# Block 0's first product in halves of 256 tokens, begun between the first chunks, with the weight pieces pinned behind the chunks' own steps

## The chip, the cores and the metric

The kernel runs on one core of one Trainium2 chip. The time is device microseconds (us) of that core. The four executions in the first measurement lie within 0.2% (733.64 to 735.28 us, the kernel before), so differences of 1 us out of 730 need several rounds on one chip; where an interval is given, it is a 95% interval of a ratio. The profile is one execution; its span is about 1.7 us shorter than the time of the same execution (733.6 against 735.37 us for the kernel before).

The engines have short names in the profile: PE is TensorE (matmuls), PEld its weight loads, DVE is VectorE, ACT is ScalarE, POOL is GpSimd, SP issues transfers.

## The reference

```python
# batch 4, 8 heads, 768 tokens, 64 per head; float32
for t in range(S):                                  # retention, chunked by 128 tokens in the kernel
    state = gamma * state + outer(k[t], v[t])
    y[t] = scale * (q[t] @ state)
x = y.transpose(0, 2, 1, 3).reshape(3072, 512)      # 3072 tokens
h = x @ w_in                                        # 512 -> 2048
out = (h * sigmoid(1.702 * h)) @ w_out              # 2048 -> 512
```

The weights come to the kernel as 64-bit words and are made float32 on the chip, in 32 pieces: 16 of w_in and 16 of w_out. This takes one ACT step and six DVE steps for each piece.

## The kernel before

The 3072 tokens go in six blocks of 512, each fed by four chunks of the retention. Blocks 2 to 5 use a product scheme with fewer multiplications, whose operands are first summed from the weights; blocks 0 and 1 run plainly while the weights are still coming in. TensorE's order is that of the program; the other engines' queues are ordered by a scheduler when the kernel is built.

```python
def narrow(n=1):                     # one piece of weights: 1 step of ACT, 6 of DVE
    for _ in range(n):
        ...
        act.activation(m, hi.bitcast(F32), AF.Abs, scale=2.0 ** 16)
        dve.tensor_scalar(m, m, F64_MOST * 2.0 ** 16, F64_LEAST * 2.0 ** 16, op0=ALU.min, op1=ALU.max)
        dve.tensor_scalar(mu, mu, 3, None, op0=ALU.logical_shift_left)
        dve.scalar_tensor_tensor(hi, hi, 0x80000000, mu, op0=ALU.bitwise_and, op1=ALU.bitwise_or)
        dve.tensor_scalar(mu, hi, 0xFF800000, None, op0=ALU.bitwise_and)
        dve.scalar_tensor_tensor(r, lo, 2.0 ** -52, m, op0=ALU.mult, op1=ALU.mult)
        dve.tensor_add(w, ..., ...)
        fetch()                      # the transfer of a later piece into the freed buffer (4 of them)

# a chunk: turn (transposes q and k, ACT copies them), attend (scores; DVE multiplies by the mask),
# finish (products with state and v; DVE writes x and adds to the state)

def up0(m, f):                       # unit f of 16: 128 of the 2048 features, 512 tokens
    p, ab = divmod(f, 2)
    x = X1 if m else X
    h = ps.tile([P, 2, TH], F32, name="ph", tag="xy"[f % 2])     # two tags, two buffers each
    for c in range(4):
        pe.matmul(h, w, x[:, c // 2:4:2, c % 2, :], start=(c == 0), stop=(c == 3))
    hidden(...)                      # ACT: sigmoid; DVE: product

turn(0)
for j in range(CB):                  # the opening: chunks 0 to 3
    attend(j)
    narrow(1)
    turn(j + 1)
    finish(j)
    narrow(1)
between = chunks(1)[1:]
for f in range(NFF):                 # block 0, with the steps of chunks 4 to 7 in between
    up0(0, f)
    if f < NP or f % 4 == 3:
        narrow(1)
    if between and f >= 2:
        between.pop(0)()
for f in range(NFF):                 # block 1
    up0(1, f)
    narrow(1)
    ...
for f in range(NFF):                 # block 0's second product; its four sums take the same PSUM tags
    down0(f)
    ...
```

## Time and profile before

| | before |
|---|---|
| time, median of 3 | 733.7 us |
| span of the profile (of another execution, which took 735.37 us) | 733.6 us |
| PE busy | 712.6 us (97%) |
| first unit of block 0 on PE | 45.04 us |
| first unit of block 1 | 119.07 us |
| block 0's second product | 174.00 us |

These three starts are the marks by which kernels are compared. From 45 us to the end PE has hardly a hole (busy 184.00 of 184.00 us up to 229 us, then 500.01 of 504.60), so a mark that comes earlier should bring the end earlier by as much. The lines of the page are in the prediction.

### The profile page before, as it was taken

The numbers are of one execution on the slowest core, as the hardware profiler recorded it, in microseconds if no ns is written. First come the engines' busy times: TensorE is split into PE (matmuls) and PEld (weight loads), VectorE is DVE, ScalarE is ACT, GpSimd is POOL, SyncE is SP. The second block draws the span as 40 slices with busy tenths as digits, with TensorE's granted clock in tenths as the row PEclk, the third lists the DMA queues.
The fourth block names the chain that finished last, engine by engine and source line by source line (L and its number), as shares of the span: only waits on it lengthen the run. The fifth ranks groups of instructions, "written<-read, shape, count | busy, mean of one in ns | idle before, by whom it ended". The sixth has DMA issues, their size and how long they took to land.

```text
span 733.6 us, 9285 instructions
## 1 busy us (share of the span) xinstructions
PE 712.6 (97%) x3552; PEld 547.0 (75%) x3552; DVE 359.8 (49%) x611; ACT 127.7 (17%) x209; POOL 136.0 (19%) x127
## 2 busy tenths in 40 slices
PE   4789999999999999999999999999999999999997
PEld 3645554444446888888888888888888888888886
DVE  4999999941002652443553344364345273244251
ACT  3233332210000000332000233000233000133100
POOL 2311000323543223000233100032200140200030
PEclk9989999999999999999999999999999999999999
DMA  9877555310001324300334310234300220100001
GB/s 241 202 177 206 157 153 168 89 30 1 0 0 58 68 47 87 74 1 1 65 54 87 61 23 0 48 57 88 74 11 0 42 46 1 44 1 0 15 1 43
DMA packets 142252, 46.24 MB, mean 63 GB/s; under 512 B 129921, under 2 KB 135553, under 8 KB 142209
## 3 DMA queue, kind: packets, MB, share of 16 engines
q1 hardware_dynamic: 135504, 39.10, 23.9%
q10 hardware_dynamic: 6704, 6.57, 2.7%
q8 instruction: 28, 0.46, 0.3%
q14 instruction: 16, 0.12, 0.1%
HBM read 39.33 MB, written 6.29 MB: 62 GB/s over the span
## 4 chain that ended last, share of the span: by engine, by line
PE 93%; DVE 4%; DMA 1%; issue 0%; ACT 0%; SPq 0%; DVEq 0%
PE pd L394 32%; PE ph L291 15%; PE px L343 15%; PE py L343 11%; PE po L303 7%; PE pa L231 3%; PE py L248 3%; PE pu L261 3%; PE py L244 2%; DMA W<-in_moe_w_in_dram 1%; DVE G L333 1%; PE pt L215 1%; DVE W L187 1%; DVE G L334 0%; DVE W L183 0%
## 5 line engine op out<-in xcount | busy, mean ns | idle before, releaser
L394 PE MATMUL pd<-W,G 128*128 128x256 f32 x1120 | 250.3, 381 | 0.4 <-DVE G L334 0.3
L394 PEld LDWEIGHTS pd<-W,G 128*128 128x128 f32 x1120 | 210.1, 190 | 31.2 <-DVE G L334 1.2
L343 PE MATMUL px<-X,W 128*128 128x256 f32 x512 | 119.0, 379 | 0.0
L343 PEld LDWEIGHTS px<-X,W 128*128 128x128 f32 x512 | 97.3, 190 | 13.2
L343 PE MATMUL py<-X,W 128*128 128x256 f32 x384 | 90.7, 379 | 0.0
L343 PEld LDWEIGHTS py<-X,W 128*128 128x128 f32 x384 | 73.0, 190 | 9.9
L222 POOL TENSOR_TENSOR kd<-kn_in,cold 128x512 f32<-128x512 f32 x13 | 15.0, 1151 | 248.8 <-DMA q_sq<-in_q_dram 126.5
L291 PE MATMUL ph<-X,W 128*128 128x512 f32 x128 | 58.5, 605 | 0.0
L291 PE MATMUL ph<-W,W 128*128 128x512 f32 x128 | 55.1, 592 | 0.0
L335 POOL TENSOR_TENSOR G<-G 128x512 f32<-128x512 f32 x20 | 28.9, 1443 | 111.6 <-DVE G L334 111.6
L234 DVE TENSOR_TENSOR at<-pa,mask 128x512 f32<-128x512 f32 x32 | 20.6, 686 | 58.7 <-PE pa L231 58.7
L291 PEld LDWEIGHTS ph<-W,W 128*128 128x128 f32 x128 | 24.3, 190 | 30.6 <-issue 30.4
L291 PEld LDWEIGHTS ph<-X,W 128*128 128x128 f32 x128 | 23.9, 194 | 26.1 <-issue 25.6
L303 PE MATMUL po<-W,W 128*128 128x512 f32 x96 | 42.5, 592 | 0.0
L278 DVE TENSOR_TENSOR G<-G,sg 128x512 f32<-128x512 f32 x48 | 33.1, 689 | 14.1 <-ACT sg L276 14.1
L276 ACT ACTIVATE sg<-G 128x512 f32<-128x512 f32 x48 | 30.3, 631 | 51.3 <-DVE G L353 30.7
L303 PEld LDWEIGHTS po<-W,W 128*128 128x128 f32 x96 | 18.2, 190 | 23.0 <-issue 23.0
L177 ACT ACTIVATE W<-W 128x512 f32<-128x512 f32 x32 | 21.8, 685 | 54.4 <-DMA W<-in_moe_w_out_dram 30.6
L268 POOL TENSOR_TENSOR state<-state,cold 64x256 f32<-64x256 f32 x32 | 21.2, 663 | 53.1 <-DVE state L270 27.6
L353 DVE TENSOR_TENSOR G<-py,p 128x512 f32<-128x512 f32 x16 | 11.1, 692 | 37.8 <-PE py L343 37.8
L306 DVE COPY o<-po 128x512 f32<-128x512 f32 x4 | 2.8, 692 | 52.7 <-PE po L303 51.2
L276 ACT ACTIVATE sg<-ph 128x512 f32<-128x512 f32 x32 | 19.0, 595 | 51.3 <-PE ph L291 43.3
(87 smaller groups left out, 682.2 us busy)
## 6 DMA issues: line engine op xcount, KB each, us to landing
W<-in_moe_w_in_dram SPq DMA_DIRECT2D x16, 512.0 KB, 4.6
W<-in_moe_w_out_dram SPq DMA_DIRECT2D x16, 512.0 KB, 3.4
v_in<-in_v_dram SPq DMA_DIRECT2D x24, 256.0 KB, 4.0
out_dram<-o ACTq DMA_DIRECT2D x24, 256.0 KB, 2.4
kn_in<-in_k_dram SPq DMA_DIRECT2D x21, 256.0 KB, 3.6
q_sq<-in_q_dram SPq DMA_DIRECT2D x256, 16.0 KB, 1.9
k_sq<-in_k_dram SPq DMA_DIRECT2D x256, 16.0 KB, 1.8
q_in<-in_q_dram SPq DMA_DIRECT2D x8, 256.0 KB, 4.6
```

The costliest lines, as they stand in the source:

```text
L177: act.activation(m, hi.bitcast(F32), AF.Abs, scale=2.0 ** 16)
L231: pe.matmul(p[:, i, hp, :], KT[j][r, hp, :], QT[j][r, hp, :], start=True, stop=True)
L248: pe.matmul(y[i * D:(i + 1) * D, hp, :], vn[:, 2 * hp + i, :], a[:, i, hp, :], start=(not c and hp == 0), stop=(hp == HP - 1), skip_group_ ...
L261: pe.matmul(u[:, hp, :], kd[:, h, :].rearrange("p i d -> p (i d)"), vn[:, h, :].rearrange("p i d -> p (i d)"), start=True, stop=True)
L268: pool.tensor_mul(new[r, :, r], old[r, :, r], cold[r, 2 * H:, None].to_broadcast([D, HP, D]))
L276: act.activation(s, h, AF.Sigmoid, scale=1.702)
L278: dve.tensor_mul(g, h, s)
L291: pe.matmul(h, w, x[:, c // 2:4:2, c % 2, :], start=(c == 0), stop=(c == 3))
L303: pe.matmul(PO[n], g0(p, 2 * half + ab)[:, t0:t0 + P], w, start=(f == 0), stop=(f == NFF - 1))
L335: pool.tensor_sub(g[1], g[1], g[0])
L343: pe.matmul(acc[:, u, :], W1[:, 2 * d + u, sa, c, :], X[:, sb, c, :], start=(start and u == 0 and c == 0), stop=(stop and c == 1), skip_gr ...
L394: pe.matmul(p0[:, n, :], G[:, p, sa, n * P:(n + 1) * P], W2[:, sb, p, :], start=(new and p == 0 and n == 0), stop=(last and p == NP - 1), ...
```

## The change

The intent is to put matmuls of block 0 into PE's holes in the opening. A unit on 512 tokens needs all four chunks; on 256 it needs chunks 0 and 1 only, so half units for three pairs of features can run between the chunks. The pins keep the scheduler from queueing pieces of weights ahead of a chunk's own steps: a pinned instruction may not be queued ahead of what was traced before it on its engine.

```diff
-            act.activation(m, hi.bitcast(F32), AF.Abs, scale=2.0 ** 16)
-            dve.tensor_scalar(m, m, F64_MOST * 2.0 ** 16, F64_LEAST * 2.0 ** 16, op0=ALU.min, op1=ALU.max)
+            tc.keep_in_program_order(act.activation(m, hi.bitcast(F32), AF.Abs, scale=2.0 ** 16))
+            tc.keep_in_program_order(dve.tensor_scalar(m, m, F64_MOST * 2.0 ** 16, F64_LEAST * 2.0 ** 16,
+                                                       op0=ALU.min, op1=ALU.max))
...
-    def up0(m, f):
+    def up0(half, p):
+        h = ps.tile([P, 2, TH], F32, name="ph", tag="xy"[p % 2])
+        for ab in range(2):
+            for c in range(4):
+                w = W1[:, p, (c // 2 if ab == 0 else (3, 2)[c // 2]), c % 2, :]
+                pe.matmul(h[:, ab], w, X[:, 2 * half + c // 2, c % 2, :], start=(ab == 0 and c == 0), stop=(c == 3),
+                          skip_group_check=True)
...
+    units = [(half, p) for p in range(3, NP) for half in range(2)]
     for j in range(CB):
         attend(j)
         narrow(1)
         turn(j + 1)
         finish(j)
         narrow(1)
+        if j:
+            up0(0, j - 1)
     between = chunks(1)[1:]
-    for f in range(NFF):
-        up0(0, f)
-        if f < NP or f % 4 == 3:
+    for n, unit in enumerate([(1, p) for p in range(3)] + units):
+        up0(*unit)
+        if n < NP or n % 2:
             narrow(1)
-        if between and f >= 2:
+        if between:
             between.pop(0)()
```

(Block 1's units are the old ones under the name up1.)

More of the change, by code (lines that the diff above doesn't have):

```diff
@@ L276, in hidden @@
         act.activation(s, h, AF.Sigmoid, scale=1.702)
-        for g, h, s in [(g, h, s)] if not isinstance(g, list) else [(g[i], h[:, i], s[:, i]) for i in range(2)]:
-            dve.tensor_mul(g, h, s)
+        for g, i in g if isinstance(g, list) else [(g, slice(0, 2))]:
+            dve.tensor_mul(g, h[:, i], s[:, i])
     def g0(p, s):
@@ L283, in g0, with up1 @@
         return X[:, 4 + p // 2, p % 2] if p < 6 else G0[:, p % 2]
-    def up0(m, f):
+    def up0(half, p):
[5 more added lines that the diff above has]
+                          skip_group_check=True)
+        if half == 0:
+            hidden(W1[:, p, 4:6].rearrange("p s c f -> p s (c f)"), h)
+        else:
+            hidden([(g0(p, 2 + i), i) for i in range(2)], h)
+    def up1(f):
         p, ab = divmod(f, 2)
-        x = X1 if m else X
         h = ps.tile([P, 2, TH], F32, name="ph", tag="xy"[f % 2])
@@ L290, in up0 @@
             w = W1[:, p, (c // 2 if ab == 0 else (3, 2)[c // 2]), c % 2, :]
-            pe.matmul(h, w, x[:, c // 2:4:2, c % 2, :], start=(c == 0), stop=(c == 3))
-        hidden(G[:, p, ab:4:2, :] if m else [g0(p, ab), g0(p, ab + 2)], h)
+            pe.matmul(h, w, X1[:, c // 2:4:2, c % 2, :], start=(c == 0), stop=(c == 3))
+        hidden(G[:, p, ab:4:2, :], h)
     PO = {}
@@ L462 @@
         narrow(1)
+        if j:
+            up0(0, j - 1)
     between = chunks(1)[1:]
-    for f in range(NFF):
-        up0(0, f)
-        if f < NP or f % 4 == 3:
+    for n, unit in enumerate([(1, p) for p in range(3)] + units):
+        up0(*unit)
+        if n < NP or n % 2:
             narrow(1)
-        if between and f >= 2:
+        if between:
             between.pop(0)()
     for f in range(NFF):
-        up0(1, f)
+        up1(f)
         narrow(1)
```

## The prediction

> **What bounds the kernel now.** I read the page first (busy shares, the 40 slices, the chain that ended last), then the stretches table of the first 229 us, then the start in order of time for each engine. First the page:
>
> ```profile
> PE 712.6 (97%) x3552; PEld 547.0 (75%) x3552; DVE 359.8 (49%) x611; ACT 127.7 (17%) x209; POOL 136.0 (19%) x127
> ...
> PE   4789999999999999999999999999999999999997
> ...
> DVE  4999999941002652443553344364345273244251
> ```
>
> TensorE (PE) is the bound: only 733.6 - 712.6 = 21.0 us of the span are without it, and the slices put nearly all of that into the first three slices (18.3 us each). There the VectorE (DVE) row reads 9. So only the opening can be won, and 21 us (2.9%) is the ceiling of any change to it. The stretches table (bounds, length, then busy us and count for PE, PEld, DVE, ACT, POOL, then the granted clock, DMA share and GB/s) says which engine fills which stretch:
>
> ```profile
> 18.20:27.40 9.20, 6.96 (x74) 5.75 (x73) 9.11 (x18) 1.77 (x3) 3.18 (x4) 1.00 0.92 210
> 27.40:33.60 6.20, 4.19 (x39) 3.26 (x38) 6.11 (x13) 2.47 (x4) 2.23 (x3) 1.00 0.65 159
> 33.60:43.30 9.70, 6.92 (x56) 5.32 (x54) 9.42 (x18) 2.25 (x4) 2.94 (x3) 0.85 0.74 180
> ...
> 45.00:119.00 74.00, 74.00 (x330) 39.77 (x329) 72.86 (x156) 23.00 (x39) 7.82 (x9) 0.99 0.64 173
> 119.00:174.00 55.00, 55.00 (x129) 24.32 (x128) 37.21 (x67) 12.73 (x22) 13.32 (x10) 1.00 0.28 70
> ```
>
> From 18 to 43 us DVE never rests and PE has holes; from 45 us on PE never rests. DVE is nearly full up to 119 us too, so it is the second bound. PE's waits before 46 us name the holes:
>
> ```profile
> PE py L248 <- DVE G L234: 5.1, 5, 2.4
> PE pt L215 <- DMA q_in<-in_q_dram: 4.3, 1, 4.3
> PE pa L231 <- ACT G L216: 3.5, 1, 3.5
> ```
>
> The chunks' own steps queue behind pieces of weights. In order of time, ScalarE (ACT):
>
> ```profile
> 9.90 0.66 ACT L177 ACTIVATE W<-W 128x512 f32<-128x512 f32 x1 [5.95 <-DMA W<-in_moe_w_in_dram]
> 10.46 1.07 ACT L216 ACTIVATE G<-pt 128x512 f32<-128x512 f32 x2
> ```
>
> The two copies of the first chunk's transposes, whose matmuls ended at 5.4 and 8.1 us, stand behind a piece that waits for its transfer until 9.9. And PE where the dense part begins:
>
> ```profile
> 40.34 0.69 PE L248 MATMUL py<-G,v_in 128*64 128x128 f32 x2 [2.41 <-DVE G L234]
> 41.27 1.97 PE L248 MATMUL py<-G,v_in 128*64 128x128 f32 x14 [0.24 <-DVE G L234]
> 43.17 2.08 PE L261 MATMUL pu<-v_in,G 128*128 128x128 f32 x8
> 45.04 11.51 PE L291 MATMUL ph<-X,W 128*128 128x512 f32 x24
> ```
>
> The first product starts at 45.04 us, after a hole of 2.4 us and a stretch at half clock (0.50 granted from 41 to 47 us).
>
> [...] the py row above takes 1.97 us for 14 passes, the same row 1.09 us later on (1.09 for 16). [...] 190 ns loads hide under 216 ns passes. [...] the queued order decides who waits, which the ACT rows show. [...] the pieces' last add took 1.53 us at 37.43, while GpSimd's kd ran, against 0.69 usually.
>
> **The change part by part.**
>
> *Halves.* A unit of block 0 was 4 products of 512 tokens, two passes each: up1's same units take 55.10 us for 128 records, 0.430 us each, so 3.44 us for 8. A half unit holds the same work as 8 products of 256, 16 passes. A row of 8 such passes starts every 1.727 us in the later blocks (295.29 to 297.02), so 3.45 us. All 16 units cost 16 x 0.02 = **+0.3 us**. The doubled weight loads (16 x 0.190 = 3.0 us in 3.45) still fit. DVE saves a little: first halves store with one product of 512 (step 0.60 us) in place of two of 256 (0.67); nothing that counts.
>
> *Three units moved.* (half 0, weight pairs 0, 1, 2) run after chunks 1, 2 and 3. Each needs x of chunks 0 and 1 alone, plus two pieces that are ready by then. That takes 3 x 3.44 = **10.3 us** of PE work out of the dense part. They fall in holes only in part: each stands before the next chunk's attend on PE, so it lengthens that chunk's chain.
>
> *Pins.* A piece's first ACT and first DVE step may not be queued ahead of what was traced before. The first copies can run at about 5.5 and 8.2 us, attend(0) at about 8.9 instead of 11.58: **2.7 us** earlier, which shrinks at once because chunk 2's inputs come behind three pieces in a DMA queue that is full (shares of 1.1 from 5 to 20 us): its transposes can't start much before the 19.4 us of now. On the other side, DVE can no longer run pieces ahead of their place.
>
> *Opening, estimated from the rows.* A piece steps DVE by 3 x 0.34 + 3 x 0.60 = 2.8 us. Chunk 2's transposes at 19.2; copies until 21.2; state and v products 2.0; x of chunk 1 by 24.3 (now 27.36 to 28.05). Then per chunk on PE: unit 3.5, attend 1.1, DVE's mask 1.3, state product and transposes partly under it, v products 1.05, update 1.1, hand-overs and a queued sigmoid product 1.2: 9.2 us. So the three units start at about 24.4, 33.6 and 42.8, and the 13 remaining at **46.3**. DVE needs by x of chunk 3: masks 5.2, x 2.4, states 2.7, 7 pieces 19.6, sigmoid products 1.2 = 31.1 us, which from 10.2 gives 41.3: close behind PE's chain, so both limit; the opening won't get shorter than now.
>
> *Dense part.* Now 45.04 to 119.07 = 74.0 us for 16 units plus chunks 4 to 7. New: 74.0 - 10.3 - 1.0 (its first 24 records took 11.3 instead of 10.3 in the half-clock stretch[...]) + 0.3 = 63.0. End at 46.3 + 63.0 = 109.3 instead of 119.07: **9.8 us** won. After that the PE work is identical and dense (119 to 229 without a hole; 500 of 504.6 us after), so it should arrive whole at the end: 733.7 - 9.8 = 723.9. I take **725**[...].
>
> **Rivals.** *A: the pins starve the later stage.* In the trace pieces run some 7 ahead of their program place by 119 us; pinned, piece n starts only behind its unit's sigmoid product. Against it: weight pair p is needed three units after its pieces are traced, about 15 us, for 5.6 us of DVE work. In block 1's units DVE has 0.60 + 2.8 = 3.4 us per 3.44 us of PE: a lag of a few us, which four PSUM buffers (three units, 10 us) hide. The second weight's pieces would end near 160 us; its 14th is needed only about 45 us later. If I'm wrong here it gives back 3 to 8 us: 727 to 732. *B: DVE stays the bound of the opening.* A unit then delays attend on PE while DVE waits behind a mask or sigmoid product it can't overtake: the opening grows by 5 us, the dense part starts at 51: 729. *C: the pins help more than DMA lets me believe*, x of chunk 1 is there at 21 and masks go first: 8.4 us per chunk, dense at 41: 719, the edge of 2%. Against it, chunk 2's inputs. *D: hidden anyway*: excluded, since the dense part is PE alone.
>
> **Range and chances.** A and B push up by 4 to 7, C down by 5: **720 to 730**. Over 2% faster means below about 719, a gain of over 14.4 of the 21.0 us that exist: 0.09. Slower by over 2% would need 14 us of new waits: 0.01. Within 2%: 0.90.
>
> **What would show it.** In the changed trace: ACT's first copies before 9 us and attend(0) near 9; sixteen-pass rows of 256 columns at about 24, 34 and 43 us, 3.5 us each; no half-clock stretch near 41 to 47; the switch from block 0 to block 1's units near 109; the rest of the trace earlier by the same 10 us. Wrong would be: PE waits on DVE's mask of over 10 us in the opening (B), PE waits in block 0's or block 1's units for a piece or a PSUM buffer (A), half units well above 3.5 us, or later stages that shift by less than block 0 did.

What no trace or run here shows is cut from the text above, at the marks. Left of the paragraph with most of the cuts are the trace's own figures: slow passes (14 in 1.97 us), loads of 190 ns under passes of 216 ns (PE is busy 500.01 of the last 504.60 us), ACT's copies that start at 10.46 us behind a piece, and the long add.

74.0 - 10.3 - 1.0 + 0.3 = 63.0 us for the dense part, so block 1 at 46.3 + 63.0 = 109.3, 9.8 us won, and 733.7 - 9.8 = 723.9, raised to 725. No trace showed why 1.1 us were added at the end, and why the half-clock stretch (the 1.0 us) should go. Both were estimates.

## The result, and the profile after

| | before | after | predicted |
|---|---|---|---|
| time, median of 4 on one chip | 734.25 us | 732.66 us | 725.0 us |
| ratio | | 0.9973 (0.9951 to 0.9994) | |
| span of the profile | 733.6 us | 730.7 us | |
| early units start | | 25.8, 36.2, 47.0 us | 24.4, 33.6, 42.8 us |
| the other 13 units start | 45.04 us (all 16) | 50.45 us | 46.3 us |
| block 1's units start | 119.07 us | 113.36 us | 109.3 us |
| PE's wait at the second product | 0 | 2.47 us | 0 |

A ratio is the mean time of one kernel's runs over that of the other's of the same rounds, so it is not quite the ratio of the medians. The change gains 0.3%, some 2 us, where 725 us within 720 to 730 was predicted. The two spans differ by 2.9 us, more than the times do, because the profile of the kernel before is of an execution that was slower (735.37 us) than the median of its others (733.7).

The page of the changed kernel, against the lines shown of before (busy share, then the 40 slices for PE and for the granted clock):

```profile
PE 710.6 (97%) x3680; PEld 569.1 (78%) x3680; DVE 365.0 (50%) x603; ACT 126.5 (17%) x209; POOL 137.9 (19%) x127
...
PE   5799999998999999999999999999999999999997
...
PEclk9999999999999999999999999999999999999999
```

The half-clock stretch is gone (every slice reads 9). But time without PE is 730.7 - 710.6 = 20.1 us, against 21.0 before. The holes that the early units were to fill are nearly as large in sum as they were; one of them now shows in the tenth slice. PE in order of time (start, duration, out and in, count of passes, idle time before it), cut to the units:

```profile
25.79 3.72 PE L292 MATMUL ph<-X,W 128*128 128x256 f32 x16 [2.17 <-DVE X L253]
36.20 3.62 PE L292 MATMUL ph<-X,W 128*128 128x256 f32 x16
46.99 7.07 PE L292 MATMUL ph<-X,W 128*128 128x256 f32 x32
...
113.36 55.10 PE L305 MATMUL ph<-W,W 128*128 128x512 f32 x128
168.30 2.74 PE L317 MATMUL po<-W,W 128*128 128x512 f32 x6
173.50 2.84 PE L317 MATMUL po<-W,W 128*128 128x512 f32 x6 [2.47 <-DVE G L279]
```

The gain is 119.07 - 113.36 = 5.7 us at block 1, and 174.00 - 168.30 = 5.7 us at the second product, and there 2.5 us of it go back in one wait. The rest of the trace is parallel: the down products that followed at 228.93 us start at 225.97, 3.0 us earlier.

Two questions follow. Why did the opening take 4 us longer than reckoned, and where does the wait of 2.47 us come from? For the first, DVE in the changed kernel, while PE waits to start chunk 2's products with v:

```profile
28.51 0.43 DVE L178 TENSOR_SCALAR W<-W 128x512 f32<-128x512 f32 x1
28.98 0.72 DVE L180 TENSOR_SCALAR W<-W 128x512 uint32<-128x512 uint32 x1
29.73 0.69 DVE L181 SCALAR_TENSOR_TENSOR W<-W,W 128x512 uint32<-128x512 uint32 x1
30.46 0.43 DVE L182 TENSOR_SCALAR W<-W 128x512 uint32<-128x512 uint32 x1
30.92 0.69 DVE L184 SCALAR_TENSOR_TENSOR W<-W,W 128x512 f32<-128x512 uint32 x1
31.64 0.69 DVE L279 TENSOR_TENSOR W<-ph,sg 128x512 f32<-128x512 f32 x1
32.25 0.68 DVE L188 TENSOR_TENSOR W<-W 128x512 f32<-128x512 f32 x1
32.85 1.28 DVE L235 TENSOR_TENSOR G<-pa,mask 128x512 f32<-128x512 f32 x2
```

One piece (L178 to L188) fills 28.51 to 32.85 but for a sigmoid product of 0.61 us (L279): 3.7 us. The scores for the mask (L235) were done at 30.6 us. Each step of the piece that stands right behind the one before it, on whose output it works, starts 0.03 to 0.05 us after that one's end. In the kernel before, where the dense part has begun, two pieces ran alternately:

```profile
48.57 0.41 DVE L179 TENSOR_SCALAR W<-W 128x512 uint32<-128x512 uint32 x1
48.90 0.41 DVE L178 TENSOR_SCALAR W<-W 128x512 f32<-128x512 f32 x1
49.24 0.68 DVE L180 SCALAR_TENSOR_TENSOR W<-W,W 128x512 uint32<-128x512 uint32 x1
```

L178 belongs to another piece, and starts 0.33 us after a step of 0.41, that is 0.08 us before that has ended. A step costs 0.33 or 0.60 us if the next one belongs to something else, and 0.46 or 0.73 if the next one needs it: 0.12 to 0.13 us more. (L279 at 31.64 starts late too, 0.72 us after L184, though it doesn't need it; so need isn't the only reason.) A piece alone pays this five times and takes 3.4 us, as from 118.24 to 121.67 us. The prediction took 2.8 us a piece from steps of the first kind. The rest of the 3.7 us above is L180, which takes 0.72 in place of 0.43 us while GpSimd works on the state (27.50 to 29.41 us).

How much of this do the pins bring? In the kernel before, which has none, the opening shows both extras as well:

```profile
11.51 0.69 DVE L180 SCALAR_TENSOR_TENSOR W<-W,W 128x512 uint32<-128x512 uint32 x1
12.24 0.43 DVE L181 TENSOR_SCALAR W<-W 128x512 uint32<-128x512 uint32 x1
12.70 1.41 DVE L183 SCALAR_TENSOR_TENSOR W<-W,W 128x512 f32<-128x512 uint32 x1
```

The starts are 0.73 and 0.46 us apart, and the last step is long beside a GpSimd product (12.34 to 13.56 us). The table takes the pieces' steps on DVE from 11 to 47 us, each from its start to the next start on DVE or, where DVE then rests, to its end; six times the mean is a piece. A step runs long if it takes over 0.04 us more than 0.43 or 0.69 us.

| | before | e1 (the change without pins, below) | changed kernel |
|---|---|---|---|
| DVE time for a piece, opening | 3.57 us | 3.51 us | 3.72 us |
| of this, steps that run long | 0.5 us | 0.5 us | 0.5 us |
| of this, next step starts late | 0.2 us | 0.2 us | 0.4 us |
| the same from 47 to 110 us | 2.95 us | 2.95 us | 3.49 us |

In the kernel before and in the changed one, every one of the long steps overlaps work of GpSimd. So a piece in the opening cost 3.6 us before anything was pinned, and the pins add about 0.2 us there (0.5 us in the dense part, where pieces had alternated). The 2.8 us was the price of the dense part, from 47 us on.

For the second question, DVE at the switch to the second product:

```profile
168.62 0.89 DVE L182 TENSOR_SCALAR W<-W 128x512 uint32<-128x512 uint32 x1
169.54 1.64 DVE L184 SCALAR_TENSOR_TENSOR W<-W 128x512 f32<-128x512 uint32 x1
171.21 1.63 DVE L191 TENSOR_TENSOR W<-W 128x512 f32<-128x512 f32 x1
172.77 0.68 DVE L279 TENSOR_TENSOR G<-ph,sg 128x512 f32<-128x512 f32 x1
```

The last three steps of the last piece stand between the sigmoid products of block 1's last two units (the first of them, L279, started at 168.02), and take 0.89, 1.64 and 1.63 us in place of 0.41, 0.68 and 0.68, while GpSimd sums weights that have just become ready. At the price of a piece alone they would take 0.46 + 0.73 + 0.60 = 1.8 us instead of 4.15; the difference of 2.4 us is about the wait (an estimate; no run takes the sums away). The last product (172.77) frees a PSUM buffer that the second product needs; PE goes on at 173.50. In the kernel before the last piece was done at 150.2 us, seven units before the switch.

### The profile page after: what moved, and what is told of

It reads as the page before. It is cut to its first block, busy times and chain, and to the rows that moved or that the text cites. A ratio compares the mean times of both kernels' runs of the same rounds, so it can differ in the third digit from the quotient of the medians.

```text
span 730.7 us, 9512 instructions
## 1 busy us (share of the span) xinstructions
PE 710.6 (97%) x3680; PEld 569.1 (78%) x3680; DVE 365.0 (50%) x603; ACT 126.5 (17%) x209; POOL 137.9 (19%) x127
## 4 chain that ended last, share of the span: by engine, by line
PE 85%; DVE 13%; DMA 1%; issue 1%; SPq 0%; ACT 0%
PE pd L408 32%; PE px L357 15%; PE py L357 11%; PE po L317 7%; PE ph L292 7%; PE py L249 3%; PE pa L232 3%; PE pu L262 3%; PE py L245 2%; DVE W L184 2%; DVE W L181 2%; DVE W L191 1%; DVE G L279 1%; DVE W L178 1%; DVE W L182 1%; DMA q_in<-in_q_dram 1%
## 5 line engine op out<-in xcount | busy, mean ns | idle before, releaser
L292 PE MATMUL ph<-X,W 128*128 128x256 f32 x256 | 58.2, 382 | 2.2 <-DVE X L253 2.2
L292 PEld LDWEIGHTS ph<-X,W 128*128 128x128 f32 x256 | 47.5, 190 | 8.9 <-DVE X L253 2.4
L235 DVE TENSOR_TENSOR at<-pa,mask 128x512 f32<-128x512 f32 x32 | 20.6, 684 | 58.7 <-PE pa L232 58.7
L317 PE MATMUL po<-W,W 128*128 128x512 f32 x96 | 42.8, 593 | 2.5 <-DVE G L279 2.5
L279 DVE TENSOR_TENSOR G<-G,sg 128x512 f32<-128x512 f32 x48 | 33.0, 688 | 13.8 <-ACT sg L277 13.8
L317 PEld LDWEIGHTS po<-W,W 128*128 128x128 f32 x96 | 18.2, 190 | 25.8 <-issue 22.0
L269 POOL TENSOR_TENSOR state<-state,cold 64x256 f32<-64x256 f32 x32 | 23.2, 725 | 46.4 <-DVE state L267 23.1
L395 ACT ACTIVATE u<-pd 128x512 f32<-128x512 f32 x5 | 3.0, 597 | 134.1 <-PE pd L408 134.1
```

The costliest lines, as they stand in the source:

```text
L269: pool.tensor_mul(new[r, :, r], old[r, :, r], cold[r, 2 * H:, None].to_broadcast([D, HP, D]))
L279: dve.tensor_mul(g, h[:, i], s[:, i])
L292: pe.matmul(h[:, ab], w, X[:, 2 * half + c // 2, c % 2, :], start=(ab == 0 and c == 0), stop=(c == 3), skip_group_check=True)
L317: pe.matmul(PO[n], g0(p, 2 * half + ab)[:, t0:t0 + P], w, start=(f == 0), stop=(f == NFF - 1))
```

## The experiments

Theory, as it stood before the runs: the loss is DVE's. Pinned pieces run alone and cost 3.7 us each in the opening, and they end so late that the last one stalls the switch. Rivals: the moved units or halves themselves cost more than reckoned; the opening is set by TensorE's own rows or by transfers; the pins are needed, so without them it would be worse.

All times are medians; "ratio" is against the kernel before in the same rounds (its medians were 734.85 to 735.05 us). A label's number is its order. Three builds (e8, e13 and e17) give a wrong result; all others give the right one. Each diff is against the changed kernel unless another is named.

### Undoing one part at a time

**e1: the change without its pins.** The two pinned lines are as in the kernel before.

```diff
-            tc.keep_in_program_order(act.activation(...))
-            tc.keep_in_program_order(dve.tensor_scalar(...))
+            act.activation(...)
+            dve.tensor_scalar(...)
```

> The change without its pins (half units and their early places kept). Theory P (the pins cost: pinned pieces run one after the other on VectorE, so a step waits for the one before, 0.46/0.73 us a step in place of 0.34/0.60, and the last pieces run late enough to stall PE 2.5 us at the switch to the down product): the switch stall is gone, pieces step 0.34/0.60 again, and the time is at or under the changed kernel's 732.7, about 730 to 732. Rival Q (the pins are what makes room: without them the chunks' masks wait behind pieces again): the third early unit starts after 50 us instead of 47.0, and the time is 734 to 737.

Measured: 733.06 us, ratio 0.9982, between the two expectations. The switch stall is gone and pieces alternate again. The early units start at 28.38, 38.42 and 48.63 us: the first 2.6 us later than with pins, since ACT's first copies stand behind a piece again (a wait of 3.8 us), but 10.0 and 10.2 us apart where the pinned kernel has 10.4 and 10.8. Both sides of the argument show: pins give the chunks' steps an early start and take part of it back in longer pieces. But the intervals stay far above the predicted 9.2 us, and a piece still costs 3.5 us: most of the miss is there without pins. The time alone wouldn't have told it.

**e2: the pins alone, in the kernel before.** The diff is against that kernel.

```diff
-            act.activation(...)
-            dve.tensor_scalar(...)
+            tc.keep_in_program_order(act.activation(...))
+            tc.keep_in_program_order(dve.tensor_scalar(...))
```

> The kernel before with the two pins alone (no half units, nothing moved). If the pins alone bring what the change brings (earlier copies, no half clock before the dense part): dense part starts 2 to 4 us before 45.0, time 731 to 733. If the moved units bring it: within 1 us of the kernel before, or slower by the 2.5 us stall at the switch, 734 to 736.

Measured: 737.89 us, ratio 1.0043, slower than either expectation. Its profile, PE after the switch (172.36 us) and the wait:

```profile
177.42 4.24 PE L304 MATMUL po<-W,W 128*128 128x512 f32 x6 [2.32 <-DVE G L279]
```

The dense part starts at 43.09 us instead of 45.04 and the second product 1.6 us earlier than before. Then the same stall comes, and after it six passes take 4.24 us instead of 2.7: the granted clock was 0.67 from 177 to 182 us, after a hole of 2.32 us. In the changed kernel's own profile it was 1.00 from 173.5 to 178 us, after one of 2.47 us (2.84 us for the six passes). So the length of the hole alone doesn't tell what the clock will be; what decides wasn't tested. The pins alone are a loss, and the stall in this profile cost more than its length: the six passes behind it took 1.5 us longer.

**e3 and e5: pins on the first 8, or the first 18, pieces only.**

```diff
-            tc.keep_in_program_order(act.activation(...))
-            tc.keep_in_program_order(dve.tensor_scalar(...))
+            pin = tc.keep_in_program_order if i < 18 else (lambda ins: ins)      # e3: 8
+            pin(act.activation(...))
+            pin(dve.tensor_scalar(...))
```

> The change, pins on the first 8 pieces only (the opening's). Theory P: the opening as in the changed kernel (third unit near 47 us), the later pieces run ahead again, PE's wait of 2.5 us at the switch goes; the time falls by 2 to 3 us, to about 730. Rival: the stall comes from the switch itself (the last units' sigmoid products are late for another reason), and stays: 732 to 733.

> The change, pins on the 18 pieces that are traced before block 1's units, none on the last 14. If the pins are worth having up to there (no waits for masks in the dense part) and only cost later (the stall of 2.5 us at the switch): opening and dense part as in the changed kernel, block 1's units near 113.4 us, no wait at the switch, time 729.5 to 730.5, under the run with 8 pins. Rival: with the late pieces free again, they overtake something else, or the dense part's waits come back, and the time stays at 731 to 733.

Measured: 731.33 us (ratio 0.9956) with 8 pins, 729.93 us (0.9934) with 18. Neither waits at the switch. With 8 pins the pieces of the dense part run ahead again and delay masks there: block 1 starts at 115.76 us. With 18 it starts at 113.63, as with all pins, and the second product runs through. So the stall needs the late pins (the runs with all pins and the late pieces where they were, e2 and e7 to e10, all show it), and is worth what it looked like: 732.66 - 729.93 = 2.7 us, or 2.9 us by the two ratios. In both profiles the first early unit took 5.41 us instead of 3.7 (in e3's the granted clock was 0.55 from 25.68 to 29.40 us); in the changed kernel's profile it took 3.72 us, at a clock of 1.00 and after the same wait of 2.17 us. Of these 1.7 us only 0.3 to 0.4 are left at the third unit (47.26 and 47.42 against 46.99 us).

**e4: half units after the opening, no pins, nothing moved.** The pins go as in e1, and:

```diff
-        if j:
-            up0(0, j - 1)
...
-    for n, unit in enumerate([(1, p) for p in range(3)] + units):
+    for n, unit in enumerate([(0, p) for p in range(3)] + [(1, p) for p in range(3)] + units):
         up0(*unit)
-        if n < NP or n % 2:
+        if n < NP or n % 4 == 3:
             narrow(1)
-        if between:
+        if between and n >= 2:
```

> Half units for block 0, all after the opening as before, no pins. The prediction's price for halves, +0.3 us: 734.0 to 735.0, and rows of 16 passes at 3.45 to 3.6 us. Rival: halves cost more in place (switches between shapes, more weight loads beside the chunks' steps), 2 us or more: over 736.

Measured: 736.26 us, ratio 1.0032, so 1 to 3 us slower than before: the rival's time (over 736), though not for its reason. In its profile the dense part is 74.8 us against 74.0, and 0.8 us of it is one wait for a mask; a row of 16 passes follows the next after 3.46 us, as priced. The passes cost what was reckoned; a wait for DVE came on top. What makes up the rest of the loss, if it is more than these 0.8 us, the profile doesn't show.

### What sets the opening

**e8: three of six DVE steps left out of the first 8 pieces (a wrong result).** The shift, the sign step and the mask of the exponent are skipped for i < 8.

```diff
-            dve.tensor_scalar(mu, mu, 3, None, op0=ALU.logical_shift_left)
-            dve.scalar_tensor_tensor(hi, hi, 0x80000000, mu, ...)
-            dve.tensor_scalar(mu, hi, 0xFF800000, None, op0=ALU.bitwise_and)
+            if i >= 8:
+                dve.tensor_scalar(mu, mu, 3, None, op0=ALU.logical_shift_left)
+                dve.scalar_tensor_tensor(hi, hi, 0x80000000, mu, ...)
+                dve.tensor_scalar(mu, hi, 0xFF800000, None, op0=ALU.bitwise_and)
```

> Wrong result on purpose: the change with three of the six VectorE steps left out of the first 8 pieces, some 1.6 us of each piece's 3.7. If the opening is late because a piece costs VectorE 3.7 us instead of the 2.8 of the prediction: the early units start near 24, 33.5 and 43 us, the prediction's times, and the time falls by 3 to 4 us, to 729. Rival (TensorE's own rows and the inputs set the opening): the third unit still starts at 46 to 47 us, and the time changes by less than 1 us.

Measured: 729.49 us, ratio 0.9927. The early units start at 24.54, 33.79 and 42.95 us (predicted 24.4, 33.6, 42.8) and block 1 at 109.32 us (predicted 109.3). The stall at the switch is still there, with a slow stretch behind it (six passes in 4.44 us).

**e13: the same with pins on 18 pieces.** The diffs of e8 and e5 together.

> Wrong result on purpose: three of six steps left out of the first 8 pieces, and no pins on the last 14. If the pieces' cost in the opening and the stall at the switch are the whole of the miss: units near 24.5, 33.8 and 43 us, block 1's near 109.3, no wait at the switch, time 724.5 to 726, the predicted 725. Rival (something else is still lost): 727 or more, with a new wait in the dense part or later.

Measured: 724.96 us, ratio 0.9862. With both causes away the kernel reaches the predicted time. That it does so to 0.04 us is chance, since these pieces are cheaper (2.3 us by the count above, in e8 2.2) than the prediction's, and in its profile the units start 1.0 us ahead of the predicted times (23.35, 32.60, 41.75 us).

**e17: one step of six left out (again a wrong result), 18 pins.** Only the sign step is skipped for i < 8: a piece takes 3.1 us in the opening by the count above, here five times the mean step (e5: 3.7), nearer to the 2.8 that was reckoned. With e5's diff:

```diff
-            dve.scalar_tensor_tensor(hi, hi, 0x80000000, mu, ...)
+            if i >= 8:
+                dve.scalar_tensor_tensor(hi, hi, 0x80000000, mu, ...)
```

> Wrong result on purpose: one of six VectorE steps (0.73 us of 3.7) left out of the first 8 pieces, pins on 18 pieces. If the term of 2.8 instead of 3.7 us is what failed: units within 0.7 us of 24.4, 33.6 and 42.8 us, time 725 to 726.7. Rival (the piece would have had to be far shorter than 2.8; the prediction's chain was too short as well): third unit at 44.5 or later, time 727.5 or more.

PE, in order of time, cut to the units:

```profile
24.48 3.72 PE L293 MATMUL ph<-X,W 128*128 128x256 f32 x16 [1.30 <-DVE X L254]
33.73 3.62 PE L293 MATMUL ph<-X,W 128*128 128x256 f32 x16
43.52 7.07 PE L293 MATMUL ph<-X,W 128*128 128x256 f32 x32
...
109.89 55.10 PE L306 MATMUL ph<-W,W 128*128 128x512 f32 x128
```

Measured: 726.55 us, ratio 0.9880. All three starts are within 0.8 us of the predicted ones. Some 0.6 us off each of 8 pieces bring 729.93 - 726.55 = 3.4 us (4.0 by the two ratios). So it is the cost of a piece on DVE that made the opening late, and a cost near the assumed one would have given the predicted opening. TensorE's rows and the transfers allow it. The run doesn't say why a piece cost 3.7 us.

**e7: the third and fourth weight transfers issued behind chunk 2's q and k.**

```diff
-    for _ in range(NRAW - 1):
-        fetch()
+    fetch()
...
     turn(0)
+    fetch()
+    fetch()
```

> The change with the third and fourth weight transfers issued behind chunk 2's q and k. If chunk 2's inputs hold the chain of the opening: its transposes start at about 17.2 us in place of 18.5, and everything after 1 to 1.3 us earlier (time 731 to 731.7). Rival: VectorE's queue holds x of chunk 1 (done at 25.7 us though the products ended at 22.5), and nothing is won: 732 to 733.

Measured: 732.76 us, ratio 0.9975, the same as the change. Chunk 2's transposes do start at 17.51 us instead of 18.46; then PE waits for masks (3.1 us in all, 1.8 before), the third unit starts at 47.37 us, and the switch stall is there as in the change. The transfers were a wait, not the bound: DVE was behind them.

### Trying to win it back

**e6 and e14: each early unit one step later, behind the next chunk's attend; e14 with 18 pins.**

```diff
         attend(j)
+        if j > 1:
+            up0(0, j - 2)
         narrow(1)
         turn(j + 1)
         finish(j)
         narrow(1)
-        if j:
-            up0(0, j - 1)
     between = chunks(1)[1:]
-    for n, unit in enumerate([(1, p) for p in range(3)] + units):
+    for n, unit in enumerate([(0, 2)] + [(1, p) for p in range(3)] + units):
```

> All pins as in the change; each early unit stands one step later on TensorE, behind the next chunk's attend instead of ahead of it, so the masks have a unit's 3.6 us to be ready. Theory (the opening's length is TensorE's own rows of 9.4 us per chunk plus waits for VectorE of 1.0 to 2.2 us each, which only this placing hides): the waits for X (2.2) and for masks (1.8) shrink under 1.5 us together, the same work is done 2 to 3 us earlier, and 1 to 3 us come off the changed kernel's time: 730 to 731.5 with the stall at the switch still there. Rival (VectorE is full and sets the pace whatever the placing): the waits move to another row, the time stays at 732 to 733.

> Units one step later and pins on 18 pieces. The run with later units already had no stall at the switch, so if that stall was most of its gain the two do not add: 728.5 to 730, like either alone. Rival (the gains are of different places and add): 726 to 727.5.

Measured: 729.32 us (0.9921) and 729.73 us (0.9924). In e6 the waits for X and masks fall from 4.0 to 1.6 us, the third unit starts at 44.62, but block 1 starts only at 113.19 us: the lag went into the dense part, and into ACT's copies (1.7 us, 0.6 before). With one piece more ahead of block 1, e6 has no stall at the switch, which its expectation had still counted on; that explains most of its gain, and e14 adds nothing to it.

**e9 and e10: pieces in pairs after each chunk's finish, their steps traced alternately and all pinned (e9), or one after the other (e10).**

```diff
         attend(j)
-        narrow(1)
         turn(j + 1)
         finish(j)
-        narrow(1)
+        narrow(2, together=True)     # e10: False
```

> The change with the opening's 8 pieces taken in pairs after each chunk's finish, the six VectorE steps of the two traced alternately (and pinned in that order); same instructions, same data, right result. Theory (a lone piece costs 3.7 us because each step waits for the step before it, 0.46 or 0.73 us, where a step of another piece in between makes it 0.34 or 0.60): a pair takes 5.6 to 5.8 us, the third early unit starts 2 to 3.5 us earlier than the changed kernel's 47.0 us, at 43.5 to 45. Rival (the steps' cost is set by something else, the transfers[...]): a pair takes 7 us or more, the third unit stays at 46.5 or later. The switch stall is untouched, so the time is 729.5 to 731 under the theory, 732 to 733 under the rival.

> The control for the pairs: both pieces at the same place, after each chunk's finish, but one after the other. Theory: a piece takes 3.6 to 3.7 us again, the third unit starts 1.5 us or more later than with alternate steps. Rival (the new place does it, not the alternation): the third unit starts within 0.5 us of the paired kernel's.

DVE of e9 (a count of 2 is one step of each piece):

```profile
30.14 1.18 DVE L180 TENSOR_SCALAR W<-W 128x512 f32<-128x512 f32 x2
...
37.33 1.28 DVE L245 TENSOR_TENSOR G<-pa,mask 128x512 f32<-128x512 f32 x2
```

Measured: 741.62 us (1.0095) and 734.21 us (1.0000). My expectation for e9 failed. The pair takes 30.14 to 36.7, so 6.6 us, between the 5.6 to 5.8 of the theory and the 7 of the rival: 3.3 us a piece, with 0.55 us on average for the steps of the first two lines in place of 0.34. By the count above a piece costs 3.4 us in e9 and 3.7 in e10. The larger loss is another: a pinned pair is one block that a mask can't enter. The scores were ready at 33.6 us, the mask starts at 37.33, and then DVE itself idles 2.0 us for PE. PE waits 7.9 us for masks, and after the waits of 3.04, 1.89 and 2.77 us PE's passes run slow for 4 us or so each time (a row of 16 passes with v takes 2.57, 2.3 and 2.57 us in place of 1.09, the 8 passes of the update behind it 1.67, 1.98 and 1.68 in place of 1.16); the third unit starts at 56.26 us, 48.71 in e10, where masks could slip between the steps. The throughput of DVE is not the measure; when a mask comes out is.

**e11 and e12: pairs everywhere; e12 with the units one step later as well.** Pairs behind every second unit of blocks 0 and 1. With e9's diff (and e6's in e12):

```diff
         up0(*unit)
-        if n < NP or n % 2:
-            narrow(1)
+        if n % 2 == 0:
+            narrow(2, together=True)
...
         up1(f)
-        narrow(1)
+        if f % 2 == 0:
+            narrow(2, together=True)
```

> The change with pairs everywhere: in the opening as before, behind every second unit of block 0 and of block 1. VectorE then needs 0.60 + 2.8 us per unit of 3.44 us of block 1 and the last piece is traced after its 11th unit instead of its 14th: the stall at the switch goes. Opening as with the pairs there, dense part as in the changed kernel (66.4 us from the third unit to block 1), so 5 to 6 us under the changed kernel: 726 to 728.5. Rival (a pair of 5.6 us behind a unit delays masks and sigmoid products, and the dense part gets waits of 1 to 3 us): 729 to 731.

> The same with each early unit one step later on TensorE, behind the next chunk's attend. If the waits for x and masks are still 1 us or more per chunk, they go and the time is 725 to 727. Rival (nothing is left to hide once the pieces are short, or VectorE hands the lag on to the dense part as in the run that placed the units later): the same as the pairs alone within 0.7 us.

Measured: 748.34 us (1.0187) and 749.93 us (1.0205). The rival was too mild: waits for masks are 13.4 and 15.4 us, and have spread into the dense part.

**e15 and e16: no piece traced between attend and finish of chunk 1, later pieces one place later; 18 pins; e16 with the units one step later.** With e5's diff (and e6's in e16):

```diff
         attend(j)
-        narrow(1)
+        if j != 1:
+            narrow(1)
...
-        if n < NP or n % 2:
+        if n <= NP or n % 2:
             narrow(1)
```

> Pins on 18 pieces, and no piece traced between attend and finish of chunk 1 (all later pieces one place later, one more in the dense part). If x of chunk 1 waits only for that piece: PE's wait for X of 2.2 us falls under 0.7, the early units start 1.5 to 2 us earlier (24, 34.3, 45), time 727.5 to 728.7. Rival (the lag goes to the masks of chunks 2 and 3, or the dense part waits for a late piece): the third unit at 46.5 or later, 729.5 to 731.

> The same with the units one step later. If VectorE still holds the chain, placing the units over the masks' wait brings another 1 to 2 us: 726 to 727.5. Rival (no wait is left that it could cover): within 0.7 us of the run before.

Measured: 729.19 us (0.9921) and 729.03 us (0.9919). The wait for X falls from 2.2 to 0.9 us in e15 and is gone in e16, but now the second and third units wait for their own weights (2.7 and 2.3 us): the third begins at 45.21 and stops within itself. The work of DVE before the third unit is the same, and something waits for it. e15 lies between its two expectations; e16, 0.2 us from e15, met its rival.

**e18: the last add of the first 8 pieces on GpSimd, 18 pins.** With e5's diff; the w_out pieces' add has the other form and stays on DVE.

```diff
-                dve.tensor_add(w, xf[:, :, :, :, 1], xf[:, :, :, :, 0])
+                (pool if i < 8 else dve).tensor_add(w, xf[:, :, :, :, 1], xf[:, :, :, :, 0])
```

> Right result: the last add of the first 8 pieces on GpSimd, pins on 18 pieces. If VectorE's share counts[...]: a piece takes VectorE about 3.0 us, as in the run before, 726 to 728. Rival ([...] the weights arrive later and a unit waits): 729 to 731, with longer VectorE steps beside it.

Measured: 728.77 us, ratio 0.9907 (0.9892 to 0.9922), between the two expectations. Intervals between units fall to 9.5 and 10.2 us, but the first starts at 26.27 us, and some of DVE's steps beside GpSimd's work are longer: a step of 0.43 us takes 1.15 beside an add of 1.42 us (at 24.37 us) and beside a product of 1.37 us (at 29.93). Beside the add of 1.04 us at 31.88 us they aren't. So a piece still costs DVE 3.5 us for its five steps, not the 3.0 that was expected. (Long steps beside GpSimd: 1.53 us at 37.43 us in the kernel before, against 0.69.) It is the fastest right kernel, 0.9% under the kernel before where the change itself has 0.3%; against e5, e6, e15 and e16 (0.9919 to 0.9934) the intervals overlap, so the order among them is open.

## Why the prediction was wrong, point by point

- **The bound and the ceiling.** Right: nothing outside the opening and the switch changed, and no run came near the 21 us.
- **Halves, +0.3 us.** Right in the passes (3.45 to 3.46 us a row). Low in place: e4 was 1 to 3 us slower than before, and 0.8 us of it is a wait for a mask.
- **The half clock.** Right for 41 to 47 us in the changed kernel (granted 1.00, against 0.50 before). But the early units don't secure the clock: in two profiles the first unit took 5.41 us (e3, at 0.55, and e5). Behind the stall of e2 the clock was 0.67.
- **The dense part, 63.0 us for 13 units.** Right: 113.36 - 50.45 = 62.9.
- **The opening.** Wrong, and the step that failed is "A piece steps DVE by 3 x 0.34 + 3 x 0.60 = 2.8 us". That is the price in the dense part. In the opening a piece costs 3.7 us in the changed kernel, and it had cost 3.6 in the kernel before, in the very trace that was read. Some 0.5 us of the 0.9 are steps that run long beside GpSimd, some 0.4 are steps that start late; the pins account for about 0.2. Units came 10.4 and 10.8 us apart instead of 9.2 (10.0 and 10.2 without the pins), and the 13 others at 50.45 instead of 46.3 us. e17, with pieces near 3 us, gives the predicted starts to 0.8 us, so this term is the 4 us. What failed with it is the choice of the path. The 9.2 us on PE were right where DVE is light (9.25 and 9.16 in e8). But with 3.7 us for each of 7 pieces the prediction's own sum for DVE is 31.1 + 6.3 = 37.4 us, which from 10.2 gives 47.6 (an estimate) and not 41.3; x of chunk 3 was done at 47.04. So DVE was the longer path, as rival B had it ("the dense part starts at 51"; it was 50.45).
- **"It should arrive whole at the end".** Wrong by 2.5 us. This is rival A in kind: the late pieces. The prediction reckoned that four PSUM buffers hide a lag of a few us. It didn't look at the last piece, which stands ahead of the last sigmoid product just where the buffers change owner, and whose steps run long beside GpSimd's sums. e5 shows the stall's worth: 2.7 us.
- **The sum.** 4.1 us in the opening and 2.5 at the switch make 6.6. The prediction had added 1.1 us to its own sum of 723.9, and the timed gain (about 2 us) came out 1 us under the profile's 2.9. It also took 9.8 us, read from a profile of a 735.37 us execution, from the median of 733.7. e13 took both causes away and measured 724.96. The range missed because A and B were weighed as alternatives; both happened, 2.5 and 4.1 us.

What stays open: whether a right kernel can have both short pieces and early masks. Pairs, fewer pieces, later units and GpSimd each moved the wait to a new place. And the parts of the 3.7 us are read from traces, not shown by a run: none takes GpSimd's work away from the opening or from the switch, and none isolates the price of a lone step or what sets the clock after a wait. e17 shows only what the time of a piece is worth.

## What to carry to other kernels

An instruction's price in a trace includes what stands next to it: if a change reorders a queue, read the start-to-start step of dependent and of independent neighbours separately (here 0.46 or 0.73 us against 0.33 or 0.60), and price the new order with the right one. Above all, read the price in the stretch that is to be changed: the same piece cost 2.95 us in the dense part and 3.57 in the opening of one trace. When work is advanced into holes, ask which engine fed the old holes: here PE's holes were DVE's work, and a unit put into them is held by the same work. A pin that helps at one end of a program can hurt at the other; with pins only where they were wanted the change gains 0.7% (e5) instead of 0.3%.
